# Float64 weights converted from their upper 16 bits, and a list schedule that picks engines by duration

## The chip, the cores and the metric

The kernel runs on one core of one Trainium2 chip. Its time is the device time of one execution in microseconds (us). Three executions of the kernel before took 1098.15, 1095.64 and 1090.09 us, so the median is 1095.64 us.

The core has five engines that run side by side and wait for one another through semaphores. TensorE (PE) multiplies matrices. VectorE (DVE), ScalarE (ACT) and GpSimd (POOL) work on elements. SyncE (SP) does no arithmetic here and issues every transfer (DMA).

## The reference, cut to what matters

Three stages follow each other: attention in chunks of 64 positions, a layer with a squared relu, and a soft mixture of eight experts.

```python
B, H, S, D = (8, 8, 576, 64)                 # 8 * 576 = 4608 rows, H * D = 512 columns
q_c, k_c, v_c = (x.reshape(B, H, 9, 64, D) for x in (q, k, v))
scores = (1 / np.sqrt(D)) * np.matmul(q_c, k_c.transpose(0, 1, 2, 4, 3))
attn = np.exp(scores - scores.max(-1, keepdims=True))
attn = attn / (attn.sum(-1, keepdims=True) + 1e-09)
x = (attn @ v_c).reshape(B, H, S, D).transpose(0, 2, 1, 3).reshape(4608, 512)
...
h = np.maximum(x @ w_in, 0.0)                # w_in 512 x 2048
x = (h * h @ w_out).astype(np.float32)       # w_out 2048 x 512
...
logits = x @ phi                             # then softmaxes over rows and slots, 8 experts
```

`w_in` and `w_out` arrive as float64, eight bytes for each weight. The chip's engines do not compute in that type, so the kernel takes the bytes apart itself and makes a float32 of each weight.

## The kernel before, in words

**Tiles and blocks.** The 4608 rows are 36 tiles of 128 rows. Attention works on one tile at a time. The middle layer works on blocks of tiles: block 0 is tile 0, block 1 is tiles 1 and 2, and every later block has three tiles. Block `NB` is a name for blocks 0 and 1 taken together.

**Chunks and steps.** The 2048 hidden columns are 16 chunks of 128, and f counts them. One step (b, f) of the middle layer has these parts. `h` multiplies a block by chunk f of `w_in` (12 matmuls, L702). `relu`, `sq` and `gh` are three passes over the result, and `gl` is what the rounding in `gh` left over. `out` multiplies gh and gl by chunk f of `w_out` (L753 to L755). Each weight is held as a large part and a small rest (`hi` and `lo` for w_in, `whi` and `wlo` for w_out). The buffers of g, gh and gl are double, so a step waits for the step two before it.

**The front and the steady part.** Before a chunk can be used, `conv(f)` has to convert it. The front of the program does the 16 conversions, the attention of tiles 0 to 8 and the first steps together. It goes in four phases (`PARTS` = (7, 12)): blocks 0 and 1 with chunks 0 to 6, block 2 with chunks 0 to 11, block NB with chunks 7 to 15, block 2 with chunks 12 to 15. That is 14 + 12 + 9 + 4 = 39 steps. After it come blocks 3 to 12, sixteen steps each, with the attention of the next tiles in between. The experts and the output end the program.

**One conversion.** `load` brings 512 KB of w_in (a = 0) and 512 KB of w_out (a = 1) into staging buffers, shifted by one byte. For each half, five operations rebuild the exponent from the top byte: `kept` clamps it (DVE, L241), `number` turns it into a number (mostly ACT, L246; POOL, L250), `rest` subtracts (POOL, L259), `lead` scales it up as an integer (ACT, L154), and `join` puts it above the shifted mantissa (DVE, L265). Then come for w_in `total`, `reduce`, `finish` (a power of two as scale), `hi` and `lo` (L309), and for w_out `whi` and `wlo` (L319). There are four pairs of staging buffers, so a chunk's load waits for `lo` and `wlo` of the chunk that had its pair before. The buffers lie where the last four chunks' `wo`, `x2T` and `lg` go later.

**What sets the order.** `list_schedule` goes through a clock of its own with a duration for each operation (`Op(engine, cost, ...)`). It hands out the ready operation of lowest rank (`RANK_T` for tiles, `RANK_F` for chunks, `RANK_S` for steps). Tables such as `ON_U`, `ON_Q`, `ON_SQ` and `ON_GL` fix which engine does an operation. The operations are written in that order. The framework then may still move instructions on each engine, except on SP, which keeps the order as written (`IN_ORDER`). Every engine works its own instructions off in order, and so does SP with the loads.

## Time and profile before

| | |
|---|---|
| median of 3 runs | 1095.64 us |
| profiled execution, its own time | 1096.36 us |
| span of its trace, first to last instruction | 1094.6 us |
| PE busy | 996.3 us, 91% of the span |
| DVE busy | 638.1 us, 58% |
| ACT busy | 523.0 us, 48% |
| POOL busy | 253.2 us, 23% |
| transfers | 112.16 MB, 102 GB/s on average |

The shares are averages over parts with different limits. The profile's line of PE in 40 slices of 27.4 us reads 4574789888, then nines to the end. So the front is read apart from what follows it. A group of rows gives the mean duration of one instruction; durations of neighbours on one engine overlap by a few hundredths of a microsecond, so busy time is a little less than count times mean.

### The profile page before, as it was taken

Reading aid. Unit: us, or ns where it says so; the run is one execution under the profiler, and the core shown is the slowest. Engines: PE = TensorE matmul, PEld = TensorE weight load, DVE = VectorE, ACT = ScalarE, POOL = GpSimd, SP = SyncE. Lnnn points to the kernel's source line nnn. Section 1 sums busy time; section 2 is a strip of 40 time slices with the busy share of each in tenths; the row PEclk is TensorE's granted clock in tenths of the full one; section 3 lists DMA queues with packets and bytes.
Section 4 is the critical chain, followed back from the end, with each engine's and each line's share of the span. In section 5 each row is a group of like instructions: output and inputs, shape, how many; then the busy total and the mean of one; then the engine's idle time right before and its main releaser. Section 6 shows DMA issues by size and latency. Waiting matters only on the chain. (4 is left out here: it accounts for less than half of the span.)

```text
span 1094.6 us, 18390 instructions
## 1 busy us (share of the span) xinstructions
PE 996.3 (91%) x7144; PEld 680.7 (62%) x7144; DVE 638.1 (58%) x1318; ACT 523.0 (48%) x966; POOL 253.2 (23%) x255
## 2 busy tenths in 40 slices
PE   4574789888999999999999999999999999999993
PEld 3453556555666676667667676666666666666352
DVE  6887986777756655656656556566565462212232
ACT  4554556522645445455555455554454544434132
POOL 3544742422311111222111111221111121000100
PEclk8666789998999999999999999999999999999895
DMA  9452544114442222223333222243442342367998
GB/s 211 104 162 44 164 89 126 39 44 63 87 88 59 59 58 59 58 59 78 69 79 67 59 58 59 58 64 69 74 85 59 78 116 87 97 202 256 293 281 237
DMA packets 248471, 112.16 MB, mean 102 GB/s; under 512 B 208064, under 2 KB 241856, under 8 KB 248384
## 3 DMA queue, kind: packets, MB, share of 16 engines
q1 hardware_dynamic: 248384, 110.98, 42.1%
q8 instruction: 56, 0.92, 0.4%
q14 instruction: 31, 0.25, 0.1%
HBM read 78.71 MB, written 9.44 MB: 81 GB/s over the span
## 5 line engine op out<-in xcount | busy, mean ns | idle before, releaser
L702 PE MATMUL hps<-xb,wi 128*128 128x384 f16 (+2 forms) x2388 | 418.6, 326 | 15.1 <-ACT g L718 6.3
L702 PEld LDWEIGHTS <-wi 128*128 128x128 f16 x2388 | 219.0, 100 | 172.5 <-issue 49.5
L753 PE MATMUL x<-wo,gh 128*128 128x512 f32 x576 | 253.9, 441 | 19.4 <-ACT gh L152 10.2
L754 PE MATMUL x<-wo,gh 128*128 128x512 f32 x576 | 229.6, 399 | 0.0
L718 ACT ACTIVATE g<-hps,inv_w 128x384 f32<-128x384 f32 (+2 forms) x191 | 108.8, 570 | 233.6 <-PE hps L702 178.0
L755 PE MATMUL x<-wo,gl 128*128 128x512 f32 x576 | 214.7, 406 | 5.7 <-DVE gl L737 5.6
L737 DVE TENSOR_TENSOR gl<-g,gh 128x384 fp32r<-128x384 f32 (+2 forms) x196 | 112.6, 578 | 103.7 <-ACT gh L152 99.7
L753 PEld LDWEIGHTS x<-wo,gh 128*128 128x128 f32 x576 | 110.1, 191 | 58.8 <-ACT gh L152 12.1
L453 POOL TENSOR_TENSOR ex<-ex,rs 128x512 f32<-128x512 f32 x29 | 30.9, 1065 | 492.6 <-DVE rs L450 473.5
L755 PEld LDWEIGHTS x<-wo,gl 128*128 128x128 f32 x576 | 107.8, 191 | 35.4 <-DVE gl L737 12.2
L754 PEld LDWEIGHTS x<-wo,gh 128*128 128x128 f32 x576 | 110.4, 192 | 17.5 <-issue 0.8
L152 ACT ACTIVATE gh<-g 128x384 fp32r<-128x384 f32 (+2 forms) x186 | 94.9, 511 | 17.5 <-PE x L754 11.3
L725 ACT ACTIVATE g<-g 128x384 f32<-128x384 f32 (+2 forms) x184 | 95.1, 517 | 4.7 <-DVE g L720 0.2
L146 DVE TENSOR_REDUCE am<-qkv 128x1 bf16<-128x512 f32 x94 | 63.4, 684 | 42.4 <-DMA qkv<-in_k_dram 27.1
L407 DVE SCALAR_TENSOR_TENSOR vbd<-qkv,as,vbd 64x512 f16<-64x512 f32 x58 | 61.2, 1055 | 16.9 <-POOL vbd L402 16.3
L402 POOL TENSOR_SCALAR vbd<-qkv,as 64x512 f16<-64x512 f32 x58 | 57.5, 991 | 37.0 <-issue 31.6
L417 DVE COPY qbd<-qkT 64x1024 f16<-64x1024 f16 x58 | 25.5, 440 | 64.5 <-DMA qkT<-qk 64.1
L259 POOL TENSOR_TENSOR stage<-stage 128x512 bf16<-128x512 bf16 x30 | 46.2, 1584 | 63.6 <-ACT stage L246 60.2
L392 DVE SCALAR_TENSOR_TENSOR qk<-qkv,as,qk 128x512 f16<-128x512 f32 x58 | 55.1, 963 | 5.7 <-ACT qk L387 5.1
L486 ACT ACTIVATE xb<-misc 128x512 f16<-128x512 f32 x29 | 17.3, 597 | 65.6 <-PE misc L483 65.6
L387 ACT ACTIVATE qk<-qkv,as 128x512 f16<-128x512 f32 x58 | 38.6, 713 | 16.2 <-DVE as L179 15.8
L491 DVE SCALAR_TENSOR_TENSOR xb<-misc,xb 128x512 f16<-128x512 f32 x29 | 20.0, 690 | 39.4 <-ACT xb L486 39.4
(199 smaller groups left out, 1227.7 us busy)
## 6 DMA issues: line engine op xcount, KB each, us to landing
unit<-in_moe_w_dram SPq DMA_DIRECT2D x37, 512.0 KB, 4.3
unit<-in_moe_w_dram SPq DMA_DIRECT2D x54, 256.0 KB, 5.9
...
```

The costliest lines, as they stand in the source:

```text
L146: dve.tensor_reduce(out=am, in_=src, axis=AX.X, op=ALU.max, apply_absolute_value=True)
L152: act.activation(out=out, in_=in_, func=ACTF.Copy)
L392: dve.scalar_tensor_tensor(out=qk16[:, 2 * a + 1], in0=flat[:, a], scalar=v["s"][:, a : a + 1], in1=qk16[:, 2 * a], op0=ALU.mult, op1=ALU. ...
L402: pool.tensor_scalar(out=dst[0], in0=vin, scalar1=v["s"][pr, 2:3], scalar2=1.0, op0=ALU.mult, op1=ALU.mult,)
L407: dve.scalar_tensor_tensor(out=dst[1], in0=vin, scalar=v["s"][pr, 2:3], in1=dst[0], op0=ALU.mult, op1=ALU.subtract,)
L702: pe.matmul(hp, wi[f][:, wl, kt], xb[:, xl, kt, :n], start=(nm == 0), stop=(nm == 3 * KT - 1))
L718: act.activation(out=r["g"], in_=r["hp"], func=ACTF.Relu, scale=inv_w[f])
L725: act.activation(out=g, in_=g, func=ACTF.Square)
L737: (dve if ON_GL.get((b, f // 4), "dve") == "dve" else pool).tensor_tensor(out=r["gl"], in0=r["g"], in1=r["gh"].bitcast(F32), op=ALU.subtract)
L753: pe.matmul(o, gh[:, c], wo[f][:, 0], start=first, stop=False)
L754: pe.matmul(o, gh[:, c], wo[f][:, 1], start=False, stop=False)
L755: pe.matmul(o, gl[:, c], wo[f][:, 0], start=False, stop=last)
```

## The change

**Conversion.** The load is shifted by two bytes, so the upper 16 bits of each weight stand by themselves as a 16-bit integer. Two operations replace five. `up` (`upper`, L237 to L256 of the new file) multiplies that integer by 2^19 into a float32 scratch, on ACT, DVE or POOL. `join` is three DVE instructions: a clamp (`tensor_scalar`, L262), a second clamp with an add into integer bits (`scalar_tensor_tensor`, L263), and the shift of the mantissa by 13 with an or (L267). The scratch `v[a]` is tile 8's `qk16` buffer and m is its `p16` buffer. So `up` of a chunk waits for `join` of the chunk before (`last`), and tile 8's `hi` waits for the last conversion (`conv_end`).

**Planner.** All tables `ON_...` go. An operation may name several engines with a duration for each, and `list_schedule` takes the engine that would end it first, within `SLACK`. Durations, ranks and `AHEAD` are new, and `PARTS` is (8, 11): blocks 0 and 1 with chunks 0 to 7, block 2 with 0 to 10, block NB with 8 to 15, block 2 with 11 to 15, 40 steps. The plan now also runs on until tile 8 is done.

```diff
-PARTS = (7, 12)
+PARTS = (8, 11)
-AHEAD = 1.1702665353509787
-ON_U = {(0, 0): 'act', (0, 1): 'act', (1, 0): 'act', ...
+AHEAD = 0.01
+HOP = 0.15
+SLACK = {'act': 3.5, 'dve': -2.69, 'pool': -0.65}
+RANK_F = [-89.74, 33.12, 35.68, 56.49, 100.85, ...
...
+def cost_of(kind, n):
+    return {
+        "read": {"act": 0.23 + 0.00088 * n, "dve": 0.08 + 0.00105 * n},
...
+        "two": {"dve": 0.07 + 0.00105 * n, "pool": 0.2 + 0.0021 * n},
...
-                out=raws[a].bitcast(I8)[:, 1 : 1 + 4096].rearrange("p (k f) -> p k f", k=4),
+                out=raws[a].bitcast(I8)[:, 2 : 2 + 4096].rearrange("p (k f) -> p k f", k=4),
...
+        def upper(a, eng):
+            h = raws[a].bitcast(I16)[:, 4 : 4 + 2048].rearrange("p (n t) -> p n t", t=4)[:, :, 0]
+            v[a] = qk16_b[(N32 + 1) % 2].rearrange("p a n -> p (a n)").bitcast(F32)[
+                :, 512 * a : 512 * a + 512
+            ]
+            if eng == "act":
+                act.activation(out=v[a], in_=h, func=ACTF.Relu, scale=2.0 ** 19, bias=least)
             else:
-                dve.tensor_scalar(half(a, 1), byte(a), -56.0, 56.0, ALU.max, ALU.min)
+                (dve if eng == "dve" else pool).tensor_scalar(
+                    v[a], h, -LEAST, 2.0 ** 19, ALU.max, ALU.mult
+                )
...
         def join(a):
+            m = p16_b[(N32 + 1) % 2].rearrange("p a n -> p (a n)").bitcast(F32)
+            s, off = 2.0 ** 19, v["off", a]
+            dve.tensor_scalar(m, v[a], (14336.0 + off) * s, -2 * off * s, ALU.max, ALU.add)
+            dve.scalar_tensor_tensor(
+                out=m.bitcast(I32), in0=v[a], scalar=(off - 14336.0) * s, in1=m,
+                op0=ALU.min, op1=ALU.add,
+            )
             dve.scalar_tensor_tensor(
-                out=word(a), in0=word(a), scalar=5, in1=top(a),
+                out=word(a), in0=word(a), scalar=13, in1=m.bitcast(I32),
                 op0=ALU.logical_shift_right, op1=ALU.bitwise_or,
             )
...
+            last = [(("f", f - 1), f"join{a}")] if f else []
+            ops[f"up{a}"] = Op(
+                {"act": 0.72, "dve": 0.65, "pool": 1.5}, None, [f"load{a}", *last], 1 + a,
+                lambda e, a=a: upper(a, e),
+            )
+            ops[f"join{a}"] = Op("dve", 1.65, [f"up{a}"], 1 + a, lambda a=a: join(a))
...
+        ops["wlo"] = Op({"pool": 1.38, "dve": 0.61}, None, ["whi"], 5, wlo)
...
+        conv_end = [(("f", NF - 1), f"join{a}") for a in range(2)] if i == N32 + 1 else []
...
             ops[f"qd{c}"] = Op(
-                on, {"dve": 0.6, "act": 0.48}[on], ["T0", *old("qk")], 1, lambda c=c: qdiag(c)
+                cost_of("read", 512), None, ["T0", *old("qk")], 1, lambda e, c=c: qdiag(c, e)
...
+            "gl": Op(cost_of("two", P * n), None, ["gh"], 0, lambda e: moe_gl(b, f, e)),
...
-        while ph < len(left) or left_s:
+        while ph < len(left) or left_s or any(avail.values()):
...
+                    at_ = max(r, free[e])
+                    if len(op.on) > 1 and min(
+                        max(r, free[x]) + c for x, c in op.on.items() if x != e
+                    ) + SLACK.get(e, 0.0) < at_ + op.on[e]:
+                        continue
```

**On SP, at the start.** The names: `stage` is a staging buffer for weights, `qkv_...` the input of a tile. Before, the rows read:

```order
L231 DMA stage<-in_moe_w_in_dram 128x4x1024
L231 DMA stage<-in_moe_w_out_dram 128x4096
L349 DMA qkv_70<-in_q_dram 64x8x64 x2
L349 DMA qkv_70<-in_k_dram 64x8x64 x2
L349 DMA qkv_70<-in_v_dram 64x8x64 x2
```

And now:

```order
L342 DMA qkv_71<-in_q_dram 64x8x64 x2
L342 DMA qkv_71<-in_k_dram 64x8x64 x2
L342 DMA qkv_71<-in_v_dram 64x8x64 x2
L342 DMA qkv_72<-in_q_dram 64x8x64 x2
L342 DMA qkv_72<-in_k_dram 64x8x64 x2
L342 DMA qkv_72<-in_v_dram 64x8x64 x2
L237 DMA stage<-in_moe_w_in_dram 128x4x1024
L237 DMA stage<-in_moe_w_out_dram 128x4096
```

The first chunk's two loads moved behind the twelve loads of tiles 0 and 1.

**On DVE, in the first phase.** `p_77` is the scratch m, `qk_73` the scratch v, `wam` belongs to a chunk, `am` and `xb` to a tile, g, gh and gl to a step. Before, a stretch reads:

```order
L241 TENSOR_SCALAR stage<-stage 128x512
L737 TENSOR_TENSOR gl<-g,gh 128x256
L737 TENSOR_TENSOR gl<-g,gh 128x128
L146 TENSOR_REDUCE am<-qkv_71 128x1
L727 TENSOR_TENSOR g<-g 128x256
L265 SCALAR_TENSOR_TENSOR stage<-stage 128x512
```

And now:

```order
L262 TENSOR_SCALAR p_77<-qk_73 128x512
L162 TENSOR_REDUCE wam<-stage 128x1
L641 SCALAR_TENSOR_TENSOR xb_79<-misc,a32s,xb_79 128x4x128
L263 SCALAR_TENSOR_TENSOR p_77<-qk_73,p_77 128x512
L267 SCALAR_TENSOR_TENSOR stage<-stage,p_77 128x512
```

The clamp and the step's passes left this engine; three instructions for each half came. Up to `lo` of the last chunk of the first phase (chunk 7) DVE has 15 such triples, no `gl`, no `sq`, no `relu`, no `wlo` and no copy of `qd`. Before, up to `lo` of chunk 6, it has 19 of L241, 17 of L265, 10 of L737 and 12 copies into `qbd`.

**On POOL, in the second phase.** `iv` and `ex` belong to a tile, `wo` to a chunk. Before:

```order
L250 TENSOR_SCALAR stage<-stage 128x512
L259 TENSOR_TENSOR stage<-stage 128x512
L319 TENSOR_TENSOR wo_1798<-stage,wo_1798 128x512
L769 TENSOR_TENSOR iv_3527<-ai 128x1
L453 TENSOR_TENSOR ex_75<-ex_75,rs 128x512
```

And now:

```order
L313 TENSOR_TENSOR wo_1416<-stage,wo_1416 128x512
L723 TENSOR_TENSOR gl<-g,gh 128x384
L313 TENSOR_TENSOR wo_1484<-stage,wo_1484 128x512
L723 TENSOR_TENSOR gl<-g,gh 128x384 x2
L313 TENSOR_TENSOR wo_1538<-stage,wo_1538 128x512
```

All `rest` instructions left POOL. 38 of the 40 steps' `gl` and all 16 `wlo` came to it.

## Rows read from the trace of the kernel before

**Rows 1.** The page: its head, and the clock that TensorE was granted, in 40 slices.

```profile
span 1094.6 us, 18390 instructions
PEclk8666789998999999999999999999999999999895
```

**Rows 2.** Busy time by stretch: length; PE, PEld, DVE, ACT, POOL; granted clock; DMA share; GB/s.

```profile
0.00:133.00 133.00, 77.00 (x719) 58.75 (x720) 104.78 (x215) 66.45 (x105) 64.56 (x68) 0.74 0.55 134
133.00:269.00 136.00, 120.69 (x694) 80.79 (x693) 101.13 (x195) 60.21 (x102) 47.16 (x42) 0.93 0.34 80
269.00:1004.00 735.00, 732.03 (x5166) 504.67 (x5164) 403.88 (x851) 370.56 (x709) 132.15 (x135) 1.00 0.36 79
```

**Rows 3.** DVE in order of time: start, us, what, [idle before <-releaser].

```profile
131.32 1.22 DVE L309 SCALAR_TENSOR_TENSOR wi<-stage,ws,wi 128x512 f16<-128x512 f32 x1
...
268.62 2.07 DVE L773 SCALAR_TENSOR_TENSOR x2sb<-x,iv,x2sb 128x512 f32<-128x512 f32 x3 [2.60 <-PE x L755]
```

**Rows 4.** PE in order of time, five places in the front.

```profile
32.37 0.26 PE L702 MATMUL hps<-xb,wi 128*128 128x128 f16 x1 [3.08 <-ACT xb L645]
...
101.43 1.11 PE L626 MATMUL misc<-ident,ex 128*128 128x128 f32 x4 [8.79 <-POOL ex L619]
...
140.24 0.96 PE L755 MATMUL x<-wo,gl 128*128 128x512 f32 x3 [0.60 <-DVE gl L737]
...
234.43 0.50 PE L753 MATMUL x<-wo,gh 128*128 128x512 f32 x1 [3.99 <-DVE gh L157]
...
257.05 0.80 PE L753 MATMUL x<-wo,gh 128*128 128x512 f32 x1 [3.31 <-DVE x2sb L773]
```

**Rows 5.** Groups on DVE, 0 to 133 us: count | busy, mean ns | idle before.

```profile
L241 DVE TENSOR_SCALAR stage<-stage 128x512 bf16<-128x512 int8 x19 | 18.4, 970 | 7.4 <-DMA stage<-in_moe_w_in_dram 6.1 <-DMA stage<-in_moe_w_out_dram 1.2
L265 DVE SCALAR_TENSOR_TENSOR stage<-stage 128x512 int32<-128x512 int32 x17 | 14.9, 879 | 6.3 <-ACT stage L154 6.2
...
L157 DVE COPY qbd<-misc 64x512 f32<-64x512 f32 x12 | 8.2, 682 | 0.1
L737 DVE TENSOR_TENSOR gl<-g,gh 128x256 fp32r<-128x256 f32 (+1 forms) x10 | 7.7, 788 | 0.0
...
L254 DVE SCALAR_TENSOR_TENSOR stage<-stage 128x512 bf16<-128x512 int8 x1 | 2.3, 2253 | 0.0
L319 DVE TENSOR_TENSOR wo<-stage,wo 128x512 fp32r<-128x512 f32 x3 | 2.0, 674 | 0.0
L727 DVE TENSOR_TENSOR g<-g 128x256 f32<-128x256 f32 x4 | 2.0, 504 | 0.0
...
L157 DVE CAST wo<-stage 128x512 fp32r<-128x512 f32 x1 | 0.4, 420 | 0.0
```

**Rows 6.** Groups on ACT and POOL, the whole span, same columns.

```profile
L246 ACT ACTIVATE stage<-stage 128x512 bf16<-128x512 int8 x21 | 28.5, 1369 | 28.7 <-DVE stage L241 28.1 <-DVE rs L616 0.4 <-DVE a32i L182 0.2
L154 ACT ACTIVATE stage<-stage 128x512 int32<-128x512 bf16 x32 | 21.7, 683 | 13.8 <-POOL stage L259 10.1 <-DVE stage L254 3.5
...
L259 POOL TENSOR_TENSOR stage<-stage 128x512 bf16<-128x512 bf16 x30 | 46.2, 1584 | 63.6 <-ACT stage L246 60.2 <-DVE stage L248 3.2
...
L453 POOL TENSOR_TENSOR ex<-ex,rs 128x512 f32<-128x512 f32 x29 | 30.9, 1065 | 492.6 <-DVE rs L450 473.5 <-ACT g L725 11.9 <-DVE ai L182 7.2
```

**Rows 7.** The chain that ended last, two pieces of the last block: start, us, what.

```profile
992.51 1.97 PE hps L702 x12
...
996.57 1.97 PE hps L702 x12
```

**Rows 8.** SP: two loads in order of time; then from its waits: total, times, longest.

```profile
8.00 1.31 SPq L349 DMA_DIRECT2D qkv<-in_k_dram  x2
...
SPq L231 <- DVE wi L309: 73.1, 8, 21.2
```

**Rows 9.** DVE under a busy POOL: one row of DVE, and line L265's min/median/max.

```profile
33.24 3.75 DVE L615 TENSOR_SCALAR su<-su 128x8 f32<-128x8 f32 x1
...
L265 DVE SCALAR_TENSOR_TENSOR stage<-stage x32: 641/709/1756, 9.5 to 236.0; 128x512 int32<-128x512 int32 x32
```

More of the change, by code (lines that the diff above doesn't have):

```diff
@@ L105 @@
     ones = const.tile([P, P], BF16, name="ones")
+    two = const.tile([P, 2], F32, name="two")
+    one, least = two[:1, 0:1], two[:, 1:2]
     phi_sb = const.tile([P, KT, NS], F32, name="phi_sb")
@@ L243, in number @@
-        def number(a):
-            on_u = ON_U.get((f, a), "act")
-            if on_u == "act":
-                act.activation(out=half(a, 0), in_=byte(a), func=ACTF.Copy)
-            elif on_u == "dve":
-                dve.tensor_scalar(half(a, 0), byte(a), 1.0, None, ALU.mult)
-            else:
-                pool.tensor_scalar(half(a, 0), byte(a), 1.0, 1.0, ALU.mult, ALU.mult)
-        def rest(a):
-            if ON_U.get((f, a), "act") == "both":
-                dve.scalar_tensor_tensor(
-                    out=half(a, 1), in0=byte(a), scalar=-56.0, in1=half(a, 1),
-                    op0=ALU.min, op1=ALU.add,
-                )
-            else:
-                pool.tensor_tensor(out=half(a, 1), in0=half(a, 0), in1=half(a, 1), op=ALU.subtract)
@@ L261, in lead @@
-        def lead(a):
-            copy(ON_LEAD.get((f, a), "act"), top(a), half(a, 1), TOP)
+        def upper(a, eng):
[5 more added lines that the diff above has]
+                act.activation(out=v[a], in_=h, func=ACTF.Relu, scale=2.0 ** 19, bias=least)
+            else:
+                (dve if eng == "dve" else pool).tensor_scalar(
+                    v[a], h, -LEAST, 2.0 ** 19, ALU.max, ALU.mult
+                )
+            v["off", a] = LEAST if eng == "act" else 0.0
@@ L669, in attention32 @@
-        ops["max"] = Op("dve", 0.6, ["qk"], 3, largest)
-        ops["less"] = Op("dve", 0.6, ["max", *old("Tp")], 3, less)
-        ops["exp"] = Op("act", 0.52, ["less"], 3, exp)
-        ops["sums"] = Op("dve", 0.8, ["exp"], 4, sums)
-        ops["normal"] = Op(on_n, {"dve": 0.6, "pool": 0.95}[on_n], ["sums"], 4, normal)
+        ops["kc"] = Op(cost_of("read", 512), None, ["T1", *old("qk")], 1, kcopy)
+        ops["qk"] = Op("pe", 1.9, ["qd0", "qd1", "kc"], 2, scores)
+        ops["max"] = Op("dve", 0.61, ["qk"], 3, largest)
@@ L674, in attention32 @@
+        ops["less"] = Op("dve", 0.61, ["max", *old("Tp")], 3, less)
+        ops["exp"] = Op("act", 0.63, ["less"], 3, exp)
+        ops["sums"] = Op("dve", 0.85, ["exp"], 4, sums)
+        ops["normal"] = Op({"pool": 1.16, "dve": 0.61}, None, ["sums"], 4, normal)
         ops["Tp"] = Op("pe", 0.5, ["normal"], 5, ptrans)
-        on = ON_Q.get((i, 3), "act")
-        ops["pc"] = Op(on, {"dve": 0.6, "act": 0.48}[on], ["Tp", *old("pv")], 6, pcopy)
+        ops["pc"] = Op(cost_of("read", 512), None, ["Tp", *old("pv")], 6, pcopy)
@@ L687, in attention32 @@
-        ops["xh"] = Op("act", 0.61, ["pv", "finish"], 8, xh)
-        ops["xl"] = Op("dve", 0.66, ["xh"], 8, xl)
+                {"pool": 0.78, "dve": 0.42, "act": 0.62}, None, ["load2", *old("pv")], 1,
+                lambda e, h2=h2: vdiag(h2, e),
+            )
+        ops["total2"] = Op("dve", 0.61, ["load2"], 0, total)
+        ops["reduce"] = Op("pe", 0.1, ["total2"], 0, reduce)
+        ops["finish"] = Op("dve", 0.45, ["reduce"], 1, finish)
+        ops["pv"] = Op("pe", 1.9, ["pc", "vd0", "vd1"], 7, pv)
@@ L1101 @@
     pool.memset(ones, 1.0)
[L1102 removed]
     pool.memset(one, 1.0)
+    pool.memset(least, LEAST * 2.0 ** 19)
     dve.tensor_tensor(out=selF, in0=ident[:NR, 0:NS], in1=ident[:NR, NS : 2 * NS], op=ALU.add)
@@ L1213, in ready @@
         def ready(task, n, op):
-            t = since[task, n] + (dma_in if op.eng == "dma" else 0.0)
+            t = since[task, n] + (dma_in if "dma" in op.on else 0.0)
             if task[0] == "s":
@@ L1293, in list_schedule @@
             else:
-                del avail[op.eng][task, n]
+                for e in op.on:
+                    del avail[e][task, n]
+                op.eng = eng
                 left_s -= task[0] == "s"
-            fin_ = t + op.cost
+            fin_ = t + op.on[op.eng]
             free[op.eng] = fin_
```

234 lines of the change are left out of this document (91 added, 143 removed).

## The prediction

> **What bounds the kernel now.** I read busy time by stretch first [rows 2]. From 269 to 1004 us PE is busy 732.03 of 735 us at full granted clock: nothing that the other engines give or lose there moves the end, as long as they keep up. The front is different. In its first 133 us PE is busy 77.0, with a granted clock of 0.74 of full speed (so partly at the lower level, 1.2 GHz), DVE 104.78, ACT 66.45 and POOL 64.56: DVE, at 79%, is the fullest. From 133 to 269 us PE is busy 120.69 of 136. The page's clock line says the same: the slices below 9 are nearly all at the left [rows 1].
>
> Then DVE and PE in order of time. The first phase's last chunk, 6, has its `lo` from 131.32 to 132.5 [rows 3], and the phase's last `out` on PE ends at 140.24 + 0.96 = 141.2 [rows 4]. On the way PE stands still for chains that run through DVE, such as 8.79 us for an `ex` that POOL gets late [rows 4]. The last store of the front's sums, on DVE, starts at 268.62 [rows 3]; from there the steady part runs. So I take DVE's work up to the last chunk of the first phase as what sets the length of the first phase, and PE's steps as what sets the rest of the front.
>
> **The change, part by part.** The sum is made against the profiled execution, 1096.36 us, which is 0.7 above the median of 1095.64.
>
> *First phase, DVE.* Up to `lo` of chunk 6 DVE loses or hands on: the clamps, 18.4 us; the old joins, 14.9; copies into `qbd`, 8.2; `gl`, 7.7; L254, 2.3; `wlo`, 2.0; L727, 2.0 [rows 5]. Together 55.5. It takes on 15 triples of three instructions on 128x512, up to `lo` of chunk 7:
> - the clamp L262, float32 in and out, has no row. Nearest are a cast of that size, 0.42, as the lower bound, and L241 with its int8 input, 0.97, as the upper. I take 0.60, nearer to the cast, since both its tensors are of plain four-byte elements.
> - L263, two float32 inputs: between L319's 0.674 (two inputs, one operation) and 0.97. I take 0.85, near to L265.
> - L267, the same form as L265: its mean, 0.88 [rows 5]. Its median of 0.709 [rows 9] is the lower bound, 0.97 the upper.
>
> A triple is then 2.33 us (1.80 to 2.91), 15 are 35.0 (27.0 to 43.7). One chunk more (its `total`, `finish` and `lo`) and one tile less (the totals of tile 7's q, k and v) come to about 2 us each and cancel. Removing 55.5 from 104.8 and adding 35.0 gives 84.3 us of DVE up to `lo` of chunk 7 (76.3 to 93.0). At the same share of 79% that is 107 us (97 to 118). The tail from `lo` to the last `out` stays 8.7 (132.5 to 141.2). So the first phase ends at 115.7 (105.5 to 126.7) instead of 141.2, with 16 steps done instead of 14.
>
> *Rest of the front.* Before, 25 steps took 141.2 to 268.6, 127.4 us. A step of three tiles takes 4.06 where PE is full [rows 7], so 101.5 are steps and 25.9 are PE's idle time (136 - 120.69 = 15.3 in the second stretch), attention products and slower clock. Now 24 steps remain: 97.4. Of the 25.9 I keep 22, as the wait of 3.99 for a `gh` of DVE [rows 4] goes with that pass to ACT. That is 119.4 (108.4 if half of the 22 is left, 123.3 if all of the 25.9 is). The front ends at 235.1, against 268.6: 33.5 us less (18.5 to 54.7, all bounds on one side). 1096.36 - 33.5 = **1063** us, the forecast, with bounds 1042 and 1078.
>
> *What I cost at nothing, and its cover.*
> - `up` on ACT: by the nearest row, L154, 0.683; above, L246, 1.369 [rows 6]. It replaces an L246 and an L154 of the same half, so ACT saves about 1.4 for each. This pays for the 12 copies into `qbd` that it takes (0.68 each by [rows 5]) and two steps' passes. ACT stays near its 66 us, under DVE's load. Without that slack its queue would delay `relu` and `sq`, and so PE.
> - POOL loses 30 `rest` of 1.584 and gets `gl` (its nearest row is L453, 1.065 for 128x512; 1.584 above) and `wlo`. Its load stays below the 64.56 of 133 that it had. It is covered while PE has other steps, which is the last rival below.
> - On SP the first chunk's two loads are moved behind twelve tile loads. A pair takes 1.31 to issue [rows 8], so six pairs put them about 8 us back. Tiles 0 and 1 get theirs earlier by the same move. Before, the first step's `h` was held by tile 0's `xb`, the attention's result, at 32.37 [rows 4], not by the weights. The cover is those 32 us of attention; if it were gone, 8 us would be lost.
> - `up` waits for the former chunk's `join`. Behind a waiting `up`, ACT's queue holds `relu`, `sq` and the `qbd` copies. In the order this wait is mostly over before `up` comes up; where it isn't, see the third rival. Tile 8's `hi` waits for the last `join`. Block 3, which has tile 8, can't start before tile 8's attention; behind the last `join` the five steps of the fourth phase, 5 x 4.06 = 20 us [rows 7], and some of the third still stand. If they don't cover that attention, PE waits for the few us left.
> - Three `wlo` fewer on DVE and three fewer operations in a conversion also free the staging slots earlier. SP waited 73.1 us for `lo`, eight times [rows 8]; these waits become shorter with the same DVE backlog that I have counted, and I don't count them twice.
>
> **A rule that speaks against it.** In the trace L265 takes 0.709 in the median and up to 1.756, and an instruction of 128x8 took 3.75 while POOL was busy [rows 9]. So something on DVE is held up at times, though the mean of 0.879 says that over half of them aren't. The Trainium skill, "SBUF — State Buffer", section "Who interferes with whom", states that a Vector instruction that reads two inputs from SBUF contends with a GpSimd instruction that reads SBUF, and that the second to issue is blocked wholly. By that rule the triples would cost more than I take; the median agrees with it only where POOL happened to be idle.
> As a mechanism of this kernel: POOL is busy 64.56 of 133, 0.49. If each DVE instruction that met a POOL instruction waited half of one (0.7, from the 1.584 and 1.065 of [rows 6]), each of the triple's three would cost 0.34 above its undisturbed 0.42 to 0.71. With 0.42 + 0.674 + 0.709 that is 2.83 a triple, 42.4 for 15, DVE 91.7, and at 79% 116; the phase ends at 125. With the same rest of 119.4 the front ends at 244, and the time is 1072.
>
> **Rivals.**
> - *DVE blocked by POOL*, just worked out: 1072. For it, the 3.75 us; against it, the median. Chance 0.12.
> - *The conversion is limited by hand-offs no longer.* The old half went DVE, ACT, POOL, ACT, DVE; the new one goes ACT, DVE. DVE sat idle 7.4 and 6.3 us ahead of L241 and L265 [rows 5]. If DVE reaches 90% of its time, `lo` of chunk 7 comes at 84.3/0.9 = 94 and the phase ends at 102; the later phases lose half of their 22 as well, 108. The front ends at 211, and the time is 1038.8. Chance 0.14.
> - *Lockstep of ACT and DVE.* One scratch v for each half and one m for both: if half of the 16 `up` of the first phase stand on ACT until a triple is done, 8 x 2.33 = 19 us of relu, sq and copies come late and PE with them. 1063 + 19 = 1082. For it, a queue that works in order; against it, that `up` is placed behind the join in the order. Chance 0.12.
> - *Loads pace the front*, so that DVE's relief is hidden: SP's 73.1 us of waits [rows 8] would then only shrink by the shorter chain of operations between a load and `lo`, 5 to 10 us in all, and the time is 1086 to 1091. Against it: DVE is full at 79% while DMA's share is 0.55 [rows 2], and the waits end with DVE's `lo`. Chance 0.10.
> - *Slower: `gl` on POOL in the steps.* `out` needs `gl`, and a step's buffers are double. With 1.1 to 1.6 for the pass where DVE took 0.788 [rows 5], and `wlo` (1.07 to 1.6) ahead of it in the queue, `gl` can end 2 us or more after `gh`. It decides once a step's chain, `relu` to `gl`, is longer than the two steps of 4.06 that the buffers allow, or 2.4 us after `gh` in the one-step order. Then 24 steps lose 2.0 and 16 smaller ones 1.0, 64 us: 1063 + 64 = 1127. Against it: POOL is idle more than half of either stretch [rows 2]. Chance 0.05.
> That the change doesn't do what it says is ruled out by the order of instructions on DVE and POOL.
>
> **How the numbers follow.** The forecast, 1042 to 1078, has 0.47; blocked 0.12, better 0.14, lockstep 0.12, loads 0.10, slower 0.05. About 1% (11 us, below 1084.7 or above 1106.6) is what a measurement of this kernel tells from no change. Faster by more: 0.47 + 0.12 + 0.14, and nearly all of lockstep's 0.12, 0.84. Within 1%: the loads' 0.10 and a rest of 0.01, 0.11. Slower: 0.05. For the range I take the better case to its middle, 1038, and at the top lockstep with something more, 1086: left out are half of the better case, most of the loads and the slower one, 0.07 + 0.08 + 0.05 = 0.20.
>
> **What would show it.** In the changed kernel's trace `lo` of chunk 7 (L303) should start near 106 us, DVE be busy near 80% until then, and the triple's means be near 0.60, 0.85 and 0.88. The phase's last `out` should end near 116 and the front's last store on DVE start near 235. The `up` on ACT should take about 0.7 and the engine's wait ahead of it be small (else lockstep); `gl` on POOL 0.5 to 1.2, with PE waiting for it seldom (else the slower case). From there on PE should be as full as before. I would be wrong in the main if DVE's share fell well below 79% with PE still waiting: then something other than DVE's load set the first phase.

## The result, and the profile after

Four executions of the changed kernel took 1050.18, 1048.85, 1047.67 and 1049.10 us, a median of 1048.97, against 1093.62 for the kernel before on the same chip (a fourth execution of it, 1091.60, came to the three named above). The ratio is 0.9589, with a 95% interval of 0.9548 to 0.9631. Repeated later beside other runs it was 0.9608 (0.9584 to 0.9632). So the change saves 43 to 45 us. I had forecast 33.5 us, a time of 1063 in a range of 1038 to 1086.

The profiled execution took 1050.18 us. Its head and its clock line, which answer to [rows 1]:

```profile
span 1048.4 us, 18446 instructions
PEclk8778999999999999999999999999999999999895
```

Busy time by stretch of the changed kernel, in the columns of [rows 2]: to the eighth `lo`, to the end of the first phase, the rest of the front, and 735 us of the steady part.

```profile
0.00:105.00 105.00, 71.08 (x736) 55.45 (x736) 80.51 (x185) 59.44 (x110) 46.97 (x64) 0.82 0.62 164
0.00:117.00 117.00, 83.08 (x815) 63.58 (x816) 89.42 (x198) 67.79 (x128) 51.80 (x70) 0.84 0.65 170
117.00:226.00 109.00, 100.65 (x612) 68.16 (x611) 76.33 (x141) 59.46 (x108) 46.94 (x41) 0.98 0.27 68
226.00:961.00 735.00, 733.23 (x5166) 505.42 (x5165) 409.39 (x865) 372.30 (x713) 132.52 (x138) 1.00 0.37 82
```

The steady part is what it was: 735 us hold the same 5166 matmuls, PE busy 733.23 against 732.03. All of the gain lies ahead of it. DVE of the changed kernel in order of time shows the two marks of [rows 3], the last `lo` of the first phase and the last stores of the front's sums:

```profile
104.28 0.75 DVE L303 SCALAR_TENSOR_TENSOR wi<-stage,ws,wi 128x512 f16<-128x512 f32 x1 [0.69 <-ACT wi L170]
...
224.01 1.41 DVE L759 SCALAR_TENSOR_TENSOR x2sb<-x,iv,x2sb 128x512 f32<-128x512 f32 x2 [5.36 <-PE x L741]
...
225.93 0.74 DVE L759 SCALAR_TENSOR_TENSOR x2sb<-x,iv,x2sb 128x512 f32<-128x512 f32 x1
```

The stores start at 224.0 instead of 268.6, 44.6 us earlier. The first phase's `out` ends near 117 instead of 141.2: 24 us of the 44.6 come there, and 20 us in the rest of the front.

DVE's triple, up to 105 us (the columns of [rows 5]):

```profile
L267 DVE SCALAR_TENSOR_TENSOR stage<-stage,p 128x512 int32<-128x512 int32 x15 | 15.0, 998 | 0.2
L263 DVE SCALAR_TENSOR_TENSOR p<-qk,p 128x512 int32<-128x512 f32 x15 | 13.5, 900 | 0.2
L262 DVE TENSOR_SCALAR p<-qk 128x512 f32<-128x512 f32 x15 | 8.4, 560 | 2.5 <-ACT qk L250 2.0
```

It takes 0.56 + 0.90 + 1.00 = 2.46 us where I had 2.33. That is a mean of two kinds. The 21 of these 45 instructions that started with POOL idle took 0.42 (L262), 0.68 (L263) and 0.68 us (L267) on average, together 1.78. The 24 that started while a POOL instruction ran took 0.69, 1.09 and 1.27. One of each kind, and the POOL instruction ahead of the first:

```profile
70.69 1.78 DVE L267 SCALAR_TENSOR_TENSOR stage<-stage,p 128x512 int32<-128x512 int32 x1
72.51 0.43 DVE L262 TENSOR_SCALAR p<-qk 128x512 f32<-128x512 f32 x1
...
70.19 1.74 POOL L313 TENSOR_TENSOR wo<-stage,wo 128x512 fp32r<-128x512 f32 x1
```

`up` on ACT, and `gl` and `wlo` on POOL, in the same stretch:

```profile
L250 ACT ACTIVATE qk<-stage,two 128x512 f32<-128x512 int16 x15 | 11.5, 768 | 11.9 <-DMA stage<-in_moe_w_out_dram 5.1 <-DMA stage<-in_moe_w_in_dram 3.2 <-issue 2.5
```

```profile
L313 POOL TENSOR_TENSOR wo<-stage,wo 128x512 fp32r<-128x512 f32 x7 | 10.5, 1495 | 1.9 <-issue 1.6 <-ACT wo L168 0.2
L723 POOL TENSOR_TENSOR gl<-g,gh 128x128 fp32r<-128x128 f32 (+1 forms) x12 | 9.8, 816 | 11.6 <-ACT gh L168 11.4
```

And PE's groups from 117 to 224 us, with what it waited for:

```profile
L688 PE MATMUL hps<-xb,wi 128*128 128x384 f16 x256 | 46.9, 334 | 4.3 <-DVE g L706 2.1 <-ACT g L704 1.5 <-ACT wi L170 0.8
L739 PE MATMUL x<-wo,gh 128*128 128x512 f32 x72 | 30.1, 420 | 0.5 <-ACT gh L168 0.3 <-ACT x2sb L768 0.2
...
L741 PE MATMUL x<-wo,gl 128*128 128x512 f32 x71 | 25.4, 405 | 0.2 <-POOL gl L723 0.2
```

`gl` on POOL holds PE up for 0.2 us in 107: the slower rival, with its 64 us, did not happen.

### The profile page after: what moved, and what is told of

Read it like the earlier page. It is cut to its first block, busy times and chain, and to the rows that moved or that the text cites. A ratio compares the mean times of both kernels' runs of the same rounds, so it can differ in the third digit from the quotient of the medians.

```text
span 1048.4 us, 18446 instructions
## 1 busy us (share of the span) xinstructions
PE 980.3 (94%) x7156; PEld 671.8 (64%) x7156; DVE 603.2 (58%) x1257; ACT 524.2 (50%) x997; POOL 240.6 (23%) x260
## 4 chain that ended last, share of the span: by engine, by line
PE 73%; DMA 6%; DVE 4%; SPq 2%; issue 1%; ACT 1%; POOL 1%; DVEq 0%; POOLq 0%; ACTq 0%
PE hps L688 30%; PE x L739 11%; PE x L741 11%; PE x L740 11%; DMA unit<-in_moe_w_dram 2%; PE ehps L1437 2%; SPq L1508 2%; PE misc L865 1%; DMA out_dram<-o 1%; DMA qkT<-qk 1%; PE misc L878 1%; PE misc L948 1%; DMA stage<-in_moe_w_in_dram 1%; PE misc L472 1%; DVE stage L267 1%
## 5 line engine op out<-in xcount | busy, mean ns | idle before, releaser
L739 PE MATMUL x<-wo,gh 128*128 128x512 f32 x576 | 250.7, 436 | 4.0 <-POOL gh L177 1.9
L740 PE MATMUL x<-wo,gh 128*128 128x512 f32 x576 | 227.7, 396 | 0.0
L704 ACT ACTIVATE g<-hps,inv_w 128x384 f32<-128x384 f32 (+1 forms) x198 | 111.1, 561 | 216.8 <-PE hps L688 177.5
L723 DVE TENSOR_TENSOR gl<-g,gh 128x384 fp32r<-128x384 f32 x162 | 91.0, 565 | 95.3 <-ACT gh L168 94.2
L739 PEld LDWEIGHTS x<-wo,gh 128*128 128x128 f32 x576 | 109.0, 189 | 40.1 <-ACT g L711 5.9
L740 PEld LDWEIGHTS x<-wo,gh 128*128 128x128 f32 x576 | 109.0, 189 | 18.3 <-issue 1.7
L168 ACT ACTIVATE gh<-g 128x384 fp32r<-128x384 f32 (+2 forms) x196 | 99.8, 511 | 21.1 <-PE x L740 15.0
L711 ACT ACTIVATE g<-g 128x384 f32<-128x384 f32 (+1 forms) x196 | 100.4, 512 | 6.3 <-DVE g L706 1.4
L395 POOL TENSOR_SCALAR vbd<-qkv,as 64x512 f16<-64x512 f32 x58 | 54.9, 947 | 38.4 <-issue 14.9
L723 POOL TENSOR_TENSOR gl<-g,gh 128x384 fp32r<-128x384 f32 (+2 forms) x38 | 39.0, 1032 | 38.0 <-ACT gh L168 33.5
```

The source lines that it names most:

```text
L168: act.activation(out=out, in_=in_, func=ACTF.Copy)
L395: pool.tensor_scalar(out=dst[0], in0=vin, scalar1=v["s"][pr, 2:3], scalar2=1.0, op0=ALU.mult, op1=ALU.mult,)
L704: act.activation(out=r["g"], in_=r["hp"], func=ACTF.Relu, scale=inv_w[f])
L711: act.activation(out=g, in_=g, func=ACTF.Square)
L723: (dve if eng == "dve" else pool).tensor_tensor(out=r["gl"], in0=r["g"], in1=r["gh"].bitcast(F32), op=ALU.subtract)
L739: pe.matmul(o, gh[:, c], wo[f][:, 0], start=first, stop=False)
```

## The experiments

The theories, as they are numbered in the expectations. 1: DVE's load sets the first phase, the theory of the forecast. 2: the length of a conversion's chain over the engines does. 3: what counts is that POOL and ACT are relieved, so that work can move to them. 4: DVE's instructions are held up while POOL works. 5: POOL's own queue. 6: DVE up to about 90 us, and PE's own work from there. "Eighth `lo`" is the start of the last `lo` of the first phase (the seventh where that phase has seven chunks). Where a number of DVE's row "by undisturbed durations" stands, it is the sum over DVE's instructions in their order, each with its duration where nothing disturbed it in the traces. Durations of neighbours overlap, so such a sum is compared with other sums of durations and not with DVE's busy time. The times are medians; the other columns come from each run's one profiled execution, which took 1056.0 us for the changed kernel's repeat, 1063.8 for pool reads, 1071.7 for quiet POOL and 1055.9 for load 1 early.

| run | time, us | ratio to before (95%) | eighth `lo` | DVE busy to it | POOL | front's end |
|---|---|---|---|---|---|---|
| before | 1094 | 1 | 131.3 | 103.1 | 63.0 | 270.7 |
| changed | 1049.0 | 0.9548 to 0.9631 | 104.3 | 79.8 | 47.0 | 226.7 |
| changed, again | 1052.2 | 0.9584 to 0.9632 | 105.5 | 79.6 | 46.6 | 228.1 |
| old conversion | 1072.3 | 0.9777 to 0.9814 | 120.9 | 92.6 | 83.9 | 242.5 |
| old planner | 1082.5 | 0.9877 to 0.9907 | 118.4 | 91.8 | 30.4 | 254.7 |
| clamp twice | 1053.2 | 0.9609 to 0.9641 | 103.5 | 84.3 | 46.6 | 225.8 |
| pass aside | 1052.2 | 0.9600 to 0.9631 | 103.4 | 82.0 | 44.7 | 226.1 |
| pool reads | 1057.3 | 0.9636 to 0.9692 | 110.0 | 86.0 | 73.0 | 234.9 |
| pool memset | 1056.5 | 0.9628 to 0.9662 | 108.4 | 82.8 | 67.1 | 230.1 |
| quiet POOL | 1066.7 | 0.9727 to 0.9771 | 119.5 | 89.8 | 24.2 | 239.2 |
| two of three | 1043.2 | 0.9505 to 0.9544 | 101.7 | 65.2 | 43.1 | 217.3 |
| up twice | 1049.3 | 0.9567 to 0.9613 | 102.3 | 77.6 | 46.0 | 224.7 |
| load 0 first | 1050.0 | 0.9569 to 0.9597 | 98.8 | 78.9 | 51.4 | 223.5 |
| load 1 early | 1063.2 | 0.9660 to 0.9727 | 109.1 | 81.6 | 49.3 | 233.7 |

**The two parts by themselves.** First the new planner with the old conversion:

```diff
-            ops[f"up{a}"] = Op({"act": 0.72, "dve": 0.65, "pool": 1.5}, None, [f"load{a}", *last], ...
-            ops[f"join{a}"] = Op("dve", 1.65, [f"up{a}"], ...
+            ops[f"kept{a}"] = Op("dve", 0.75, [f"load{a}"], ...
+            ops[f"num{a}"] = Op({"act": 1.36, "pool": 1.5}, None, [f"kept{a}"], ...
+            ops[f"rest{a}"] = Op("pool", 1.45, [f"num{a}"], ...
+            ops[f"lead{a}"] = Op("act", 0.68, [f"rest{a}"], ...
+            ops[f"join{a}"] = Op("dve", 0.7, [f"lead{a}"], ...
```

> The changed kernel's planner, phases and ranks with the five-operation conversion of the kernel before (one byte's shift, clamp on DVE, number on ACT or POOL, rest on POOL, lead on ACT, join on DVE, with durations from the trace of before). Theory 1, DVE's load sets the first phase: with undisturbed durations DVE's row of instructions up to lo of chunk 7 sums to 87.7 us here, against 80.3 in the changed kernel, where that lo came at 104.3; so lo comes near 114, the first phase ends near 126 and the time is near 1059 (1052 to 1068): most of the gain is the planner's. Theory 2, the hand-offs of a conversion between engines set it: five of them as before, so the first phase ends near 140 and the time is near 1085 or above. Theory 3, the conversion's relief of POOL and ACT is what the planner lives on: with 30 rest of 1.58 back on POOL and 30 us back on ACT these engines become late, and the time is 1070 to 1080.

Then the kernel before with the new conversion:

```diff
-            ops[f"kept{a}"] = Op("dve", 0.34, [f"load{a}"], 1 + a, lambda a=a: kept(a))
...
-            ops[f"lead{a}"] = Op(on, {"act": 0.52, "dve": 0.34, "pool": 0.66}[on], [f"rest{a}"], ...
-            ops[f"join{a}"] = Op("dve", 0.6, [f"lead{a}"], 1 + a, lambda a=a: join(a))
+            ops[f"up{a}"] = Op("act", 0.52, [f"load{a}", *last], 1 + a, lambda a=a: upper(a))
+            ops[f"join{a}"] = Op("dve", 1.54, [f"up{a}"], 1 + a, lambda a=a: join(a))
```

> The kernel before with its tables, ranks and phases, and with the new conversion alone (up on ACT always, three instructions on DVE). Theory 1, DVE's load: DVE's instructions up to lo of chunk 6 sum to 98.6 us with undisturbed durations, against 98.3 in the kernel before, so the first phase ends near 141 as before and the time stays within 10 us of 1093. Theory 2, hand-offs: a half goes over two engines instead of five, so lo of chunk 6 comes 10 us or more earlier and the time is 1080 or less. Theory 3, POOL's and ACT's relief: it counts only when DVE's work is moved there, so about 1090 as with theory 1, with POOL's busy time of the first 133 us down from 64.6 to about 25.

The planner alone gives 22 us, the conversion alone 11.5, both 43 to 45: some 10 us come only from the two together. (The new planner kept the ranks and phases that stand with the new conversion; with others the split could differ.) The first run's time, 1072.3, is theory 3's: with `rest` back POOL is busy 83.9 of 121 us. DVE's share up to the eighth `lo` stayed at 77%, and DVE was held up too: its durations add up to 108.0 us there, 20 above the 87.7 undisturbed. The second run went against theory 1 as I had put it. DVE has nearly the same row of instructions as before (98.6 against 98.3 us undisturbed), but the first phase is 13 us shorter. DVE's busy time in the two kernels, up to the last `lo` of the phase; first before, then the old planner with the new conversion:

```profile
0.00:131.00 131.00, 75.45 (x713) 57.92 (x713) 102.78 (x212) 64.45 (x102) 62.66 (x67) 0.75 0.56 136
```

```profile
0.00:118.00 118.00, 67.25 (x698) 52.83 (x698) 91.40 (x216) 47.48 (x85) 30.00 (x46) 0.80 0.62 150
```

DVE's 212 instructions took 102.78 us beside a POOL that was busy 62.66; 216 took 91.40 beside one busy 30.00. The share of DVE stayed the same (78%, 77%). So work that is the same by undisturbed durations is shorter when POOL is quieter: the durations in the two traces add up to 125.6 us before and to 106.2 here. The `lo` came 13 us earlier, as theory 2 had it too (10 us or more). But a shorter chain alone would leave DVE's busy time as it was, and the two runs below that lengthen the chain (clamp twice, up twice) moved that `lo` by no more than 2 us, and to the earlier side.

**More on DVE, on the chain and beside it.**

```diff
             dve.tensor_scalar(m, v[a], (14336.0 + off) * s, -2 * off * s, ALU.max, ALU.add)
+            dve.tensor_scalar(m, v[a], (14336.0 + off) * s, -2 * off * s, ALU.max, ALU.add)
```

> The changed kernel with the first clamp (L262) issued twice in each conversion: DVE gets 15 more instructions of 0.56 us, 8.4 us, up to lo of chunk 7, and 32 in all, each of them on the conversion's own chain. Theory 1, DVE's load: at a share of 77% the first phase ends 11 us later and the time is near 1060 (1056 to 1062). Theory 2, length of the chain: 0.56 us each for the 8 chunks' first halves, 4 to 5 us, so near 1053. If neither counts (loads or PE pace the front), within 2 us of 1049.

```diff
                 op0=ALU.logical_shift_right, op1=ALU.bitwise_or,
             )
+            dve.tensor_scalar(m, m, 0.0, 0.0, ALU.max, ALU.add)
```

> The changed kernel with one more DVE pass of the same size behind each conversion's last instruction, over the scratch m, whose result nobody reads: the same 15 x 0.56 us of load on DVE up to lo of chunk 7, but no link of the chain from load to lo. Theory 1, DVE's load: as much as the doubled clamp, near 1060 (1056 to 1062). Theory 2, length of the chain: next to nothing, 1049 to 1051.

Both came out near the changed kernel's repeat, 1052.2: by the ratios they cost 1 to 4 us, and the intervals overlap. The added pass beside the chain, and what L267 took in that run:

```profile
L267 DVE SCALAR_TENSOR_TENSOR stage<-stage,p 128x512 int32<-128x512 int32 x15 | 11.7, 778 | 0.1
...
L271 DVE TENSOR_SCALAR p<-p 128x512 f32<-128x512 f32 x15 | 7.7, 515 | 0.2
```

7.7 us were added, but DVE's busy time up to the eighth `lo` rose by 2.2 only (79.8 to 82.0). L267 gave back 3.3 (0.998 to 0.778 each), since they met POOL's instructions less, and other instructions the rest. The eighth `lo` came at 103.4. Theory 1's 11 us are refuted: DVE's load has no fixed price in the changed kernel.

**POOL louder and quieter.**

```diff
+            scr = qk16_b[N32 % 2].rearrange("p a n -> p (a n)").bitcast(F32)
+            if f < 8:
+                pool.tensor_tensor(out=scr[:, :1], in0=wo[f][:, 1, :1].bitcast(F32), ...)
+                pool.memset(scr, 0.0)
+                for _ in range(2):
+                    pool.tensor_tensor(out=scr[:, :512], in0=scr[:, :512], in1=scr[:, 512:], op=ALU.subtract)
```

> The changed kernel with work on POOL that nobody uses: behind wlo of each of the chunks 0 to 7 a small instruction, a memset and two TENSOR_TENSOR of 128x512 float32 on a scratch in SBUF, some 16 x 1.3 + 8 x 1.4 = 32 us more on POOL in the first phase. Theory 1, DVE's load alone: DVE's instructions are the same, so the eighth lo stays within 2 us of 104.3. Theory 4, DVE's two-input instructions are held up while POOL reads SBUF (in old_planner DVE's instructions up to lo of chunk 6 were the same by undisturbed durations, 98.6 against 98.3, but took 91.8 us instead of 103.1, with POOL at 30 us instead of 63): L263's and L267's means rise from 0.90 and 1.00 to 1.1 and more, DVE's busy time up to the eighth lo rises by 5 us or more (0.3 us for each us of POOL), and that lo comes 6 to 12 us later; time 1055 to 1062. Theory 5, POOL's own queue: gl and the normalisation stand behind the added work, so the first phase ends later by 5 to 15 us without longer DVE instructions.

Against that kernel:

```diff
-                    pool.tensor_tensor(out=scr[:, :512], in0=scr[:, :512], in1=scr[:, 512:], op=ALU.subtract)
+                    pool.memset(scr, 0.0)
```

> As pool_reads, but with memsets of 128x1024 (which read nothing) in the place of the 16 TENSOR_TENSOR, of about the same length (L147 took 1.38), at the same places in POOL's order. Theory 4, DVE held up by POOL's reads: L263's and L267's means stay near 0.90 and 1.00, and the eighth lo comes earlier than in pool_reads by 5 us or more. Theory 5, POOL's queue: the same delay as pool_reads, within 2 us. Theory 1: no change against the changed kernel.

And against the changed kernel again:

```diff
-            "gl": Op(cost_of("two", P * n), None, ["gh"], 0, lambda e: moe_gl(b, f, e)),
+            "gl": Op(only(cost_of("two", P * n), "dve"), None, ["gh"], 0, lambda e: moe_gl(b, f, e)),
...
-        ops["wlo"] = Op({"pool": 1.38, "dve": 0.61}, None, ["whi"], 5, wlo)
+        ops["wlo"] = Op({"dve": 0.61}, None, ["whi"], 5, wlo)
```

> The changed kernel with gl and wlo only on DVE; the planner orders anew. POOL loses 54 passes (about 39 of gl in all, 21 of wlo). Theory 1, DVE's load by undisturbed durations: DVE's row up to the eighth lo sums to 100.1 us instead of 80.3, so that lo comes near 130 and the time is 1065 to 1075. Theory 4, POOL's reads hold DVE up: the triple's mean falls from 2.46 to 1.85 to 2.0 us, which gives back 8 to 9 us for 19 triples, so that the eighth lo comes near 118 and the time is 1055 to 1062.

The triple with the two loud POOLs, reads first, then memsets, then with the quiet one, each up to the eighth `lo`:

```profile
L263 DVE SCALAR_TENSOR_TENSOR p<-qk,p 128x512 int32<-128x512 f32 x15 | 14.5, 964 | 0.2
L267 DVE SCALAR_TENSOR_TENSOR stage<-stage,p 128x512 int32<-128x512 int32 x15 | 14.4, 957 | 0.2
L262 DVE TENSOR_SCALAR p<-qk 128x512 f32<-128x512 f32 x15 | 10.1, 676 | 2.7 <-ACT qk L250 2.1
```

```profile
L263 DVE SCALAR_TENSOR_TENSOR p<-qk,p 128x512 int32<-128x512 f32 x15 | 13.6, 907 | 0.2
L267 DVE SCALAR_TENSOR_TENSOR stage<-stage,p 128x512 int32<-128x512 int32 x15 | 13.5, 902 | 0.2
L262 DVE TENSOR_SCALAR p<-qk 128x512 f32<-128x512 f32 x15 | 12.7, 849 | 2.2 <-ACT qk L250 1.7
```

```profile
L263 DVE SCALAR_TENSOR_TENSOR p<-qk,p 128x512 int32<-128x512 f32 x19 | 15.1, 794 | 0.2
L267 DVE SCALAR_TENSOR_TENSOR stage<-stage,p 128x512 int32<-128x512 int32 x19 | 14.5, 764 | 0.1
L262 DVE TENSOR_SCALAR p<-qk 128x512 f32<-128x512 f32 x19 | 8.2, 431 | 6.6 <-ACT qk L250 6.2
```

A triple takes 2.60, 2.66 and 1.99 us, against 2.46 in the changed kernel. So POOL does lengthen DVE's instructions, and the quiet one gives back 0.47 for each triple: the `lo` came at 119.5, as theory 4 had it (118), and not at 130. The time, 1066.7, is theory 1's (1065 to 1075) and not theory 4's (1055 to 1062); the front's end came 11 to 13 us after the changed kernel's. With the loud POOLs 20 to 26 us more on POOL added only 0.14 to 0.20 to a triple, and nearly all of it on L262, which rose from 0.56 to 0.68 and 0.85. The means of L263 and L267 did not rise to the 1.1 that I had expected with reads.

The single instructions show why. Two memsets ran on POOL here (the last row), beside one instruction of each kind:

```profile
75.66 0.68 DVE L267 SCALAR_TENSOR_TENSOR stage<-stage,p 128x512 int32<-128x512 int32 x1
76.38 0.99 DVE L262 TENSOR_SCALAR p<-qk 128x512 f32<-128x512 f32 x1
...
75.13 1.96 POOL L323 MEMSET qk<- 128x1024 f32 x2
```

L267 and L263, which have two inputs, took their undisturbed 0.67 to 0.69 us wherever only a memset overlapped them (six times in this trace), and L262, with one input, waited for memsets as well as for reads. In the seven traces that have all three instructions in this plan, each L263 or L267 of more than 0.76 us, 167 in all, had started while POOL ran an instruction that reads, and ended 0.54 to 0.56 us after that one did. So each waits until the POOL instruction is over: theory 4, by the single instruction. How often one meets the other decides the mean, and more work on POOL did not make L263 and L267 wait longer on average. The eighth `lo` came 3 to 6 us later in both loud runs, part of it by POOL's queue (theory 5); the two are not separated further. The quiet POOL also shows that the planner's move was worth it: 1066.7 us, 14 to 18 more.

**Less on DVE.** Here the second clamp is left out.

```diff
-            dve.scalar_tensor_tensor(
-                out=m.bitcast(I32), in0=v[a], scalar=(off - 14336.0) * s, in1=m,
-                op0=ALU.min, op1=ALU.add,
-            )
```

> The changed kernel without the second clamp (L263): each conversion on DVE has two instructions instead of three, so the weights are wrong; everything else runs as it did. DVE loses 16 instructions of 0.90 us up to the eighth lo, 14 us. Theory 1, DVE's load paces the whole first phase: at a share of 77% the phase ends 18 us earlier and the time is near 1032. Theory 6, DVE paces it only until about 90 us and PE from there on (in the changed kernel PE is idle 33 us before 92 us and hardly at all after it; the two runs with 8 us more on DVE cost nothing): PE gets its chunks earlier, but its own 83 us of work stay, so about half of it, 5 to 9 us, and the time is 1041 to 1046, with PE's idle time still before 90 us and no more than 25.

The time fell by 6 to 9 us, as theory 6 said, but not where it said. DVE was relieved of 14.6 us up to the eighth `lo`, which came 2.6 us earlier; the third to sixth came at 69.9, 78.4, 85.3 and 91.6, where the changed kernel has 69.3, 78.5, 84.0 and 92.4. DVE was no longer full anywhere; from 52 to 79 us, changed kernel first, then this one:

```profile
52.00:79.00 27.00, 18.86 (x208) 14.18 (x206) 26.46 (x47) 16.70 (x32) 17.71 (x18) 0.77 0.49 131
```

```profile
52.00:79.00 27.00, 18.25 (x206) 13.54 (x204) 18.08 (x39) 14.67 (x29) 17.80 (x20) 0.86 0.46 118
```

DVE is busy 26.46 of 27 us in one and 18.08 in the other, and both kernels do about as many matmuls. PE, in the same order of kernels, shows where the chunks stay. The reduction of the third chunk's maximum (L185) comes up in PE's queue at nearly the same time, behind `out` and attention products, and the step that waits for the chunk 6 to 7 us after it, when the scale has gone through the queues of DVE and ACT.

```profile
62.26 0.18 PE L185 MATMUL misc<-wam,ones 128*128 128x1 bf16 x1
...
69.36 0.82 PE L688 MATMUL hps<-xb,wi 128*128 128x128 f16 x4 [5.02 <-ACT wi L170]
```

```profile
63.63 0.18 PE L185 MATMUL misc<-wam,ones 128*128 128x1 bf16 x1
...
69.94 3.93 PE L684 MATMUL hps<-xb,wi 128*128 128x128 f16 x24 [5.47 <-ACT wi L170]
```

PE is idle for 5 us ahead of that step, and DVE isn't full: neither one's load fixes these times. What fits is the order that was written for all engines together, with the planner's durations; no run with a new plan for the shorter join was made, so that stays a reading. For the phase's last chunks SP's order is a part of it. Its loads there, changed kernel first, and ACT's `up` behind the load of `w_out` in the changed kernel:

```profile
82.18 1.27 SPq L342 DMA_DIRECT2D qkv<-in_k_dram  x2
83.89 1.16 SPq L237 DMA_DIRECT2D stage<-in_moe_w_out_dram  x1
85.15 8.47 SPq L237 DMA_DIRECT2D stage<-in_moe_w_in_dram  x2
```

```profile
82.73 1.27 SPq L338 DMA_DIRECT2D qkv<-in_k_dram  x2
84.45 0.33 SPq L237 DMA_DIRECT2D stage<-in_moe_w_out_dram  x1
84.89 7.84 SPq L237 DMA_DIRECT2D stage<-in_moe_w_in_dram  x2
```

```profile
89.39 0.75 ACT L250 ACTIVATE qk<-stage,two 128x512 f32<-128x512 int16 x1 [4.71 <-DMA stage<-in_moe_w_out_dram]
```

Both kernels issue the eighth chunk's half of `w_in` at about 85 us, behind the loads of a tile that went out late, though DVE has 14.6 us less to do in the second. In the eight traces with this plan that load went out at 79 to 90 us, and the eighth `lo` came 17 to 21 us behind it, in one (pass aside) 24. So late in the phase these times go with a load, and not with DVE's work; no run moved that load by itself. The gain came later: the sixteenth `lo` at 182.8 instead of 192.9, and PE with 98.36 of 100 us busy in the rest of the front.

**ACT, and the loads.** Here `up` is issued twice.

```diff
                 act.activation(out=v[a], in_=h, func=ACTF.Relu, scale=2.0 ** 19, bias=least)
+                act.activation(out=v[a], in_=h, func=ACTF.Relu, scale=2.0 ** 19, bias=least)
```

> The changed kernel with up issued twice on ACT: 0.77 us more in the chain from load to lo of each half and 12 us more on ACT in the first phase, nothing on DVE. Theory 1 and 6, DVE and then PE pace the phase and ACT at 59 of 105 us has room: within 3 us of 1051. Theory 2, the chain or ACT's queue (relu, sq and gh stand behind up): 6 to 12 us, near 1060.

11 us more on ACT (70 of 102 us up to the eighth `lo` instead of 59 of 104) and a longer chain cost nothing measurable. Then the order of the loads is changed:

```diff
-        def add(task, ops, rank):
+        def add(task, ops, rank0):
             for x, (n, op) in enumerate(ops.items()):
+                rank = rank0
+                if "dma" in op.on and task[0] == "f" and task[1] in (0,):
+                    rank = -300.0
```

> The changed kernel with the two loads of chunk 0 issued first on SP, ahead of the twelve loads of tiles 0 and 1, as in the kernel before; the planner orders anew around it. The first lo then comes near 15 us instead of 29. If that move costs nothing, as I held, because the first step waits for tile 0's attention: no gain, and tile 0's attention 1.3 us later, 1050 to 1053. If DVE's early idle time is worth something (0 to 26 us it is busy 57%), the work done there is missing from the full stretch after it, and the time is 1045 to 1048.

And, against that kernel:

```diff
-                if "dma" in op.on and task[0] == "f" and task[1] in (0,):
-                    rank = -300.0
+                if "dma" in op.on and task[0] == "f" and task[1] in (1,):
+                    rank = -80.0
```

> The changed kernel with the two loads of chunk 1 issued right behind those of chunk 0 (in the changed kernel they stand on SP behind loads of tiles 2 and 3, which wait for their buffers, and go out at 29.8 and 30.5 us). Theory 6, DVE's early idle time is what is left to win in the first phase: the second lo comes at 35 to 40 us instead of 49.6, the eighth 3 to 6 us earlier, and the time is 1044 to 1048. Theory 1 with DVE's load unchanged gives the same direction, since less of DVE's time is idle. If PE's own work from 92 us on decides alone, within 2 us of 1051.

With chunk 0 first the first `lo` came at 13.0 instead of 29.2, the second at 55.1 instead of 49.6. The eighth came at 98.8, 5.5 us earlier, and the front's end 3 us earlier, but the time was the same within the intervals: the move on SP is hidden, as forecast. With chunk 1 early the second `lo` came at 40.7, but the third at 72.5 and the eighth at 109.1. In the profiled execution, the fastest of its four at 1055.9, the next loads of weights went out at 38.5 instead of 29.8, behind loads of tiles that waited for their buffers. The early chunk was paid for by the next ones; my 3 to 6 us were wrong in sign. None of these kernels beats the changed one with all of its work done.

## Why the prediction was right, point by point

- *What bounds.* Right: the front alone changed, the steady part kept its 5166 matmuls in 735 us.
- *DVE's sum in the first phase.* 84.3 us forecast, 80.5 measured; 107 us for the `lo`, 104.3 to 105 measured; share 79% forecast, 77% measured. The triple was 0.13 us dearer than I took it, and the 7 us of small groups that I had left out more than made up for it. The phase's end, 115.7, was near 117. That the triple came so near is in part luck. I took its prices from means of the kernel before, such as 0.88 for L265, that held waiting behind POOL: with POOL idle L265 takes 0.68 and the new triple 1.78. Waiting was no term of the sum. By sums of durations up to the phase's last `lo`, the traces lie some 27 us above the undisturbed row before and 11 after (125.6 against 98.3, 90.9 against 80.3), so part of DVE's relief is less waiting, and not less work.
- *The rest of the front* is the term that was mis-sized: 119.4 forecast, 107 measured (117 to 224), just below its own lower bound of 108.4, and with it nearly all of the 13 us between 1063 and 1050. I kept 22 of 25.9 us of idle time, attention and slow clock; 9.7 were left (107.1 - 97.4). Three things fell. PE's idle time between the phase's last `out` and the stores went from 14.7 to 7.2 us (127.40 - 112.69 and 107.00 - 99.82 in the rows below). `out` got faster with the clock, which was 0.98 instead of 0.93: group means of 0.420, 0.394 and 0.405 against 0.452, 0.414 and 0.420, times 72 instructions of each, 4.8 us. And the second phase had begun earlier: of the 24 steps' 288 matmuls of `h` 256 were left after 117 us, so it was 2.7 steps ahead, where before it was one (288 of 300 left). That is 1.7 times 1.97 us [rows 7], 3.3 us. Together these are 15.6 of the 16.2 us. The prediction had no term for steps that begin ahead of the phase's end.

The kernel before, 141.2 to 268.6 us, and the changed one, 117 to 224 us, then PE's groups of the kernel before:

```profile
141.20:268.60 127.40, 112.69 (x651) 75.64 (x650) 92.61 (x185) 57.57 (x95) 42.25 (x37) 0.93 0.29 71
117.00:224.00 107.00, 99.82 (x608) 67.90 (x607) 74.34 (x137) 59.16 (x108) 46.94 (x41) 0.98 0.28 70
```

```profile
L702 PE MATMUL hps<-xb,wi 128*128 128x384 f16 x288 | 54.1, 337 | 6.3 <-ACT g L718 6.3
L753 PE MATMUL x<-wo,gh 128*128 128x512 f32 x76 | 34.4, 452 | 7.6 <-DVE gh L157 4.0 <-DVE x2sb L773 3.3 <-POOL gh L161 0.3
L754 PE MATMUL x<-wo,gh 128*128 128x512 f32 x76 | 31.5, 414 | 0.0
L755 PE MATMUL x<-wo,gl 128*128 128x512 f32 x76 | 27.8, 420 | 0.8 <-DVE gl L737 0.8
```

- *The step from DVE's load to the phase's length.* The number held, the reason only in part. Over five plans (before, changed, old conversion, old planner, quiet POOL) DVE's share up to the last `lo` is 75 to 79%, so length and DVE's busy time go together; which of them sets the other these runs do not show. Within one written order they do not: +4.5 us of busy time moved that `lo` by -0.8, -14.6 us by -2.6. The forecast was made across two plans, where the share held. Whether a plan made anew for a lighter conversion would win all of it was not tried.
- *DVE blocked by POOL*, to which I gave 0.12: the mechanism is there, in a smaller size. The rival started from an undisturbed triple of 1.80, which the trace bears out (1.78), and added 1.03 for waiting; the trace has 0.68. The Trainium skill ("SBUF — State Buffer", "Who interferes with whom") says that a Vector instruction with two inputs in SBUF contends with a GpSimd instruction that reads SBUF, and not with one that only writes it. The traces agree on both: an L267 behind a reading `wlo` took 1.78 us, an L267 beside a memset 0.68.
- *Lockstep*: the 32 `up` on ACT waited 5.1 us in all for a `join`, 0.3 of them in the first phase, and a doubled `up` cost nothing.

```profile
L250 ACT ACTIVATE qk<-stage,two 128x512 f32<-128x512 int16 x32 | 24.5, 767 | 24.9 <-DMA stage<-in_moe_w_in_dram 9.6 <-DMA stage<-in_moe_w_out_dram 6.9 <-DVE p L263 5.1
```

- *Loads*: two reorderings gave nothing or a loss. But the same row has 16.5 us of ACT's waits ended by loads, and the phase's last `lo` came 17 to 21 us behind a late one in seven of eight traces. In this the rival had a part, though the gain was not hidden as it said. *gl on POOL*: 0.2 us.
